# Attention with a gated feed-forward on one core: the projection weights' powers of two applied at the PSUM eviction instead of in the exponential

## The chip, the cores and the metric

The kernel runs on 1 core of one Trainium2 chip. The metric is device time in microseconds (us) from the start to the end of one execution; the number quoted for a kernel is the median of its runs. Besides the runs that are only timed there is one profiled execution, from which every row and trace answer comes.

## The reference

`x` is 2048 x 512, there are 32 heads of 128, with 2048 cached keys and values each, and a feed-forward layer of width 1792. All inputs are bf16.

```python
xn = layernorm(x)                                    # eps 1e-5, no weights
q = (xn @ wq) split into 32 heads of 128
scores = q @ k_cache^T * 128 ** -0.5                 # per head, 2048 x 2048
o = softmax(scores) @ v_cache
s = (heads of o side by side) @ wo                   # 2048 x 4096 @ 4096 x 512
h = relu(xn @ w1 + b1) ** 2
g = silu(h @ w2 + b2)
out = x + s * g
```

## The kernel before

**Tiling.** The 2048 queries are cut into four query blocks of 512 (`j` = 0 to 3). A block passes through all 32 heads, so there are 128 units, numbered `g` = 32 j + head; the text calls such a unit a head. A head has eight steps, numbered `pi` = 8 g + k from 0 to 1023, and a step covers 256 keys:

- two score matmuls of 128 x 512 on TensorE (PE) write keys by queries into half of the PSUM tile `psA`, which has two such halves (`gen_scores`);
- one exponential of 128 x 1024 on ScalarE (ACT) reads that half and writes bf16 into one of eight slots of `pT`. No maximum is subtracted. The score matmuls two steps later need the half that it frees;
- two steps later the value matmuls read the slot (`gen_pv`).

**Two forms of the value product.** In most heads V is the stationary operand and the 512 columns of `pT` move (`gen_pv_b`, 16 matmuls of 512 columns for a head). The sum of the exponentials, which the softmax divides by, is then made beside PE: for a step either VectorE (DVE) reduces the `pT` slot (`den_part`), or GpSimd (POOL) first adds its two halves into `h_sum` (`part_add`) and DVE reduces that (`part_half`). Then come a sum, a small transpose, two trips through device memory and a reciprocal, ACT's copy of the result from PSUM (`o_col`) and a POOL multiplication into `oT`. In the other heads V moves and `pT` is stationary (`gen_pv`, 64 matmuls of 129 columns for a head, the 129th being ones, which gives the sum directly); DVE copies the result (`o_un`), POOL scales it and a DMA transposes it into `oT`. A head of this kind spares DVE and POOL the reductions. Its V is loaded in pieces of 128 elements rather than 512.

**Projection.** In block 0 each head's queries come from four matmuls of 128 x 512 and one DVE copy into `qt_sb`. From block 1 on (g >= 32) two heads are projected together by `job_pair`, with seven block products instead of eight, in Strassen's manner: sums and differences of weight blocks in fp16, which POOL prepares once during blocks 0 and 1 (`wp_sums`), times sums and differences of the activations. So that the fp16 sums keep their precision, each head's weights are first multiplied by a power of two taken from their largest magnitude (`chunk_scale`, `wp_mul`), and this factor has to be undone later. `sc_q[:, head, 1]` holds the factor, and `sc_q[:, head, 0]` its inverse times 128 ** -0.5. In the kernel before, the exponentials of blocks 1 to 3 take `sc_q[:, head, 0]` as their scale, a per-partition operand (a pointer); those of block 0 have the constant 128 ** -0.5.

The products of `job_pair` land in the two banks of `psF`, in steps `n` = 0 to 6. Steps 0, 2 and 4 are copied from PSUM into `u_t` (`keep`), steps 1, 4 and 6 are added to such a copy into `qt_sb` (`add`), step 5 is copied straight into `qt_sb`. Each of these seven evacuations frees a bank for a later step.

**Order.** A Python scheduler writes out each engine's instruction order before the launch. It keeps a planned clock per engine, `_cost` giving each instruction a planned duration. `PE` runs the steps with other jobs between (projections, feed-forward, output projection), at most two or three matmul groups a step (`fill_one`), and a pair's step starts only if its bank is planned to be free (`soon`). DVE's and POOL's other work is put where the planned clocks leave room (`fill_dve`, `fill_pool`). `at_a(g)` decides whether V moves in head g: always in the first two and the last three heads, otherwise where DVE's planned debt (`owed`) passes `A_OWED` and none of the three heads before has V moving. So a change of `_cost` moves instructions on all engines. `copy_off` picks ACT for a copy if ACT's planned clock is within `ACT_ROOM` (500 ns) of PE's, otherwise DVE; in the kernel before all 192 of its copies go to DVE.

Of the kernel before, what the change touches and what calls it, by code (L numbers as in the profile page):

```python
# [5 lines left out]
ACT = mybir.ActivationFunctionType  # L6
ALU = mybir.AluOpType
# [54 lines left out]
def _cost(name, fn):  # L62
    f, k = fn.func, fn.keywords
    n = _elements(k["out"])
    if name == "PE":
        return n / 2.4 + 2.5, n / 2.4 + 166
    if name == "ACT":
        return n * 0.83 + 70, n * 0.83 + 172
    if name == "POOL":
        if f in (_tt, _stt) and n > 1:  # L70
            c = n * 2.3 + 55 if k["out"].tensor.name in ("oT", "out_t") or (
                k["out"].dtype == F16) else n * 2.05 + 60
            return c, c + 50
        return (500, 560) if f is _tt else (n + 100, n + 150)
    if f in (_reduce_t, _abs_max):
        n = _elements(k["in_"])
    elif f is _reduce:
        n = _elements(k["in_"]) * 1.3 + 35
    elif f is _recip:
        n = n * 3.1  # L80
    elif f in (_bn_stats,):
        n = _elements(k["in_"])
    elif f is _ts and _in_sbuf(k["in0"]):
        n = n / 2
    elif f is _tt and k["out"].dtype == F16:
        n = n / 2
    return n / 0.96 + 70, n / 0.96 + 150


# [224 lines left out]
def bass_recurrent_scan__mha_block_cached__dense_activation_squared_relu__prompt_kernel(  # L314
# [14 lines left out]
    _, H, Sk, Dh = A_k_cache.shape  # L329
# [10 lines left out]
    SM_SCALE = float(Dh) ** -0.5  # L340
# [3 lines left out]
    HC = 8  # L344
# [12 lines left out]
    LATE_U = 700  # L357
# [14 lines left out]
    AC = S.eng("ACT")  # L372
    DV = S.eng("DVE")
# [4 lines left out]
    def E(eng, fn, deps=(), inc=True, late=LATE):  # L378
        if eng is DV and backfill[0] is not None:
            backfill[0](S.ready(deps) + late)  # L380
        return S.emit(eng, fn, deps=deps, inc=inc)

    sb = nc.alloc_sbuf_tensor
    NSL, NSW, NQS, NPT, NOT, NOC, NHS = 3, 4, 5, 8, 21, 5, 3
# [19 lines left out]
    u_t = sb("u_t", [P, 3, HB], F32)  # L404
# [5 lines left out]
    sc_q = sb("sc_q", [P, H, 2], F32)  # L410
# [95 lines left out]
    def choose(g, stationary_v):  # L506
# [3 lines left out]
        else:  # L510
# [7 lines left out]
                            op0=ALU.is_equal), deps=[t_idf])  # L518
# [240 lines left out]
    t_cs = {}  # L759
# [38 lines left out]
    def chunk_scale(q):  # L798
        def small(o, i, s1, s2, op0, op1, deps, cast=False):
            out, in0 = mx_t[0:HC, o:o + 1], mx_t[0:HC, i:i + 1]  # L800
            if cast:
                out, in0 = out.bitcast(I32), in0.bitcast(I32)
            return E(DV, partial(_ts, out=out, in0=in0, scalar1=s1, scalar2=s2, op0=op0, op1=op1),
                     deps=deps)

        t = E(DV, partial(_reduce_max, out=mx_t[0:HC, 0:1], in_=mx_h[0:HC, :]),
              deps=[t_mg[q], t_cs.get(q - 1)])
        t = small(1, 0, 1e-30, 1.6e38, ALU.max, ALU.min, [t])
        t = small(2, 1, 0x7F800000, None, ALU.bitwise_and, ALU.bypass, [t], True)
        t2 = E(DV, partial(_recip, out=mx_t[0:HC, 4:5], in_=mx_t[0:HC, 2:3]),  # L810
               deps=[t, t_cp.get(q - 1)])
        t_cs[q] = small(3, 2, SM_SCALE, None, ALU.mult, ALU.bypass, [t, t2, t_cp.get(q - 1)])

    def scale_put(q):
        t_cp[q] = S.emit_dma(SP, partial(_dma, out=sc_scr[q], in_=mx_t[0:HC, 3:5]), sl_cp,
# [83 lines left out]
    def gen_scores(pi):  # L899
        g, k = divmod(pi, NPR)  # L900
        s2, i = pi % 2, g % NSL
        assert t_kfill[g] is not None and t_evac[g] is not None
        t = None
        if g == 0:
            qt, b = divmod(pi, 2)
            for c in range(NKT // 2):
                t = E(PE, partial(_mm_shared, out=psA[:, s2 * 1024 + c * P:s2 * 1024 + (c + 1) * P],
                                  lhsT=kT[:, 0, (b * NKT // 2 + c) * P:(b * NKT // 2 + c + 1) * P],
                                  rhs=qt_sb[:, 0, qt * P:(qt + 1) * P], start=True, stop=True),
                      deps=[t_k0[b], t_q0[qt], t_exp[pi - 2] if pi >= 2 else t_b1[0]],  # L910
                      inc=(c == NKT // 2 - 1))
        else:
            for n in range(2):
                tt = 2 * k + n
                t = E(PE, partial(_mm, out=psA[:, s2 * 1024 + n * 512:s2 * 1024 + (n + 1) * 512],
                                  lhsT=kT[:, i, :].rearrange("p (k t) -> p t k", t=NKT)[:, tt, :],
                                  rhs=qt_sb[:, g % NQS, :],
                                  start=True, stop=True),
                      deps=[t_exp[pi - 2] if pi >= 2 else None, t_kfill[g], t_evac[g],
                            t_bankF[0] if pi == 0 else None],  # L920
                      inc=(n == 1))
        if k == NPR - 1:
            t_S_last[g] = t
        if pi >= NPT and is_b((pi - NPT) // NPR) and pi - NPT not in t_part:
            x = [x for x in quiet if x[1].func is den_part and x[1].args[0] == pi - NPT][0]
            run_quiet(x)
        cuts = [0, QB, 2 * QB] if pi == NPAIR - 1 else [0, 2 * QB]
        for c0, c1 in zip(cuts, cuts[1:]):
            t_exp[pi] = E(AC, partial(_act, out=pT[:, pi % NPT, c0:c1],
                                      in_=psA[:, s2 * 1024 + c0:s2 * 1024 + c1],  # L930
                                      func=ACT.Exp,
                                      scale=SM_SCALE if g < H else sc_q[:, g % H, 0:1]),
                          deps=[t, t_PV[pi - NPT] if pi >= NPT else None, t_part.get(pi - NPT),
                                None if g < H else t_sq[g % H // HC]])
            t_exp0.setdefault(pi, t_exp[pi])

    t_exp0 = {}
# [420 lines left out]
            return t_evac[g]  # L1358
        return NDC, mm, evac

    def copy_off(out, in_, deps):
        if max(AC.t, S.ready(deps)) <= PE.t + ACT_ROOM:
            return E(AC, partial(_act, out=out, in_=in_, func=ACT.Copy), deps=deps)
        return E(DV, partial(_copy, out=out, in_=in_), deps=deps, late=LATE_U)

    def job_pair(g):
        j, p = g // H, g % H // 2
        js = j % 2 * QB
        w, ws = parts(wq_pair[p % 2])

        def x_of(k, q):
            return lambda c: xnT[:, 2 * k + c, js + q * HB:js + (q + 1) * HB]

        def s_of(i):
            return lambda c: xs_t[:, i, c, :]

        steps = [(0, w[0, 0], x_of(0, 0), True), (1, w[0, 1], x_of(1, 0), True),
                 (0, ws[1], s_of(1), False), (1, ws[0], s_of(0), True),
                 (0, ws[2], s_of(2), False), (0, w[1, 1], s_of(3), False),
                 (1, ws[3], x_of(1, 1), False)]  # L1380

        def q_of(g, q):
            return qt_sb[:, g % NQS, q * HB:(q + 1) * HB]

        def mm(n, bank):
            y, lhs, rhs, start = steps[n]
            b = bank ^ y
            place = bankF(b)[:, 0:HB]
            for c in range(2):
                t = E(PE, partial(_mm_shared, out=place, lhsT=lhs[:, c, :], rhs=rhs(c),  # L1390
                                  start=start and c == 0, stop=c == 1),
                      deps=[t_wqfill[g], t_xs[j], t_bankF[b]] + tok_xT[j], inc=c == 1)

            def keep(i):
                t_us[i] = copy_off(u_t[:, i, :], place, [t, t_us[i]])
                return t_us[i]

            def add(x, q, i):
                t_us[i] = E(DV, partial(_tt, out=q_of(x, q), in0=place2, in1=u_t[:, i, :],
                                        op=ALU.add),  # L1400
                            deps=[t, t_us[i], t_S_last[x - NQS]], late=LATE_U)
                return t_us[i]

            place2 = bankF(bank ^ 1)[:, 0:HB]
            if n in (0, 2, 4):
                t_bankF[b] = keep(n // 2)
            if n == 1:
                t_bankF[b] = add(g, 0, 0)
            if n == 4:
                t_bankF[b ^ 1] = add(g + 1, 1, 2)  # L1410
            if n == 5:
                t_bankF[b] = t_evac[g + 1] = copy_off(q_of(g + 1, 0), place,
                                                      [t, t_S_last[g + 1 - NQS]])
            if n == 6:
                t_bankF[b] = t_evac[g] = add(g, 1, 1)
                t_pdone[g] = t_xuse[j] = t
                n_xuse[j] += 1

        def evac(bank, step):
            bank_no[0] ^= 1  # L1420
            if g % H == H - 2 and j + 1 < NQB:
                x_sums(j + 1)
            return t_bankF[bank]
        return 7, mm, evac
# [494 lines left out]
```

## Time and profile before

| | us |
|---|---|
| median of 3 runs | 1223.91 (1222.3 to 1225.86) |
| the profiled execution, its own time | 1221.36 |
| its span, first to last instruction | 1219.5 |
| PE busy | 1205.0 |
| ACT busy | 1148.5 |
| DVE busy | 1089.2 |
| POOL busy | 1072.4 |
| mean granted TensorE clock | 1.000 |

PE is TensorE's matmuls, PEld its weight loads, which overlap matmuls; DVE is VectorE, ACT ScalarE, POOL GpSimd and SP the queue that issues most DMAs. A group's row has its source line, engine, operation, what it writes and reads (out<-in) with shapes, the count; then busy us and mean ns of one; then the engine's idle us just before such instructions and who ended it. Most matmuls have the line of a helper, L231 or L236, so groups are told apart by tile: `psA` scores, `psO` values, `psF` everything else. A line of the wait view reads: who waited, for whom, us in total, times, longest. A line of the stretches has the window, then busy us (and instructions) of PE, PEld, DVE, ACT and POOL, the granted clock, the DMA engines' share and GB/s.

### The profile page before, as it was taken

To read this page: it belongs to the slowest core of one execution; us is meant where nothing else is said; L and a number is where in the kernel's file an instruction comes from. 1 tells how busy PE (TensorE), PEld (TensorE's weight loads), DVE (VectorE), ACT (ScalarE), POOL (GpSimd) and SP (SyncE) were. 2 spreads that over 40 slices of the span, in tenths; PEclk is the share of its full clock that TensorE was granted. 3 is DMA by queue.
4 is the path that set the end of the run, shared out by engine and by line. 5 is a ranking of instruction groups with operands and counts; after the bars stand their busy time and mean duration, and the time that the engine had idled before them with its cause. 6 is when DMAs were issued, how large, how long until landed. Compare 5 with 4: busy or idle time off the path is not lost.

```text
span 1219.5 us, 20766 instructions
## 1 busy us (share of the span) xinstructions
PE 1205.0 (99%) x6716; PEld 699.6 (57%) x6845; DVE 1089.2 (89%) x2064; ACT 1148.5 (94%) x1188; POOL 1072.4 (88%) x1027
## 2 busy tenths in 40 slices
PE   9999999999999999999999999999999999999999
PEld 7555555555665555566566565655555565555566
DVE  5999899998989999977988999798999999989973
ACT  7999999999999999999999999999999999999995
POOL 2999899999879899978977979799999989999973
PEclk9999999999999999999999999999999999999999
DMA  9799999899889799897987879787797887878871
GB/s 218 170 210 213 222 216 208 204 203 225 217 203 240 190 224 208 199 214 170 208 175 177 205 184 210 165 203 181 168 209 179 196 194 166 205 174 188 189 174 42
DMA packets 501023, 236.27 MB, mean 194 GB/s; under 512 B 387985, under 2 KB 477329, under 8 KB 500913
## 3 DMA queue, kind: packets, MB, share of 16 engines
q1 hardware_dynamic: 498816, 230.85, 84.5%
q0 software_dynamic: 1424, 3.81, 1.0%
q8 instruction: 54, 0.88, 0.3%
q14 instruction: 57, 0.46, 0.1%
q10 hardware_dynamic: 672, 0.26, 0.1%
HBM read 152.87 MB, written 11.55 MB: 135 GB/s over the span
## 4 chain that ended last, share of the span: by engine, by line
PE 89%; DVE 3%; ACT 3%; POOL 2%; issue 1%; DMA 0%; SPq 0%; POOLq 0%; ACTq 0%
PE psA L231 33%; PE psO L231 28%; PE psF L231 17%; PE psF L236 6%; PE psO L236 5%; ACT pT L240 2%; DVE d_part L299 2%; POOL h_sum L244 1%; ACT o_col L240 0%; DMA kT<-in_A_k_cache_dram 0%; DVE h2T L254 0%; DVE r_t L250 0%; PE psA L236 0%; POOL wq_sb L244 0%; POOL oT L244 0%
## 5 line engine op out<-in xcount | busy, mean ns | idle before, releaser
L240 ACT ACTIVATE pT<-psA,sc_q 128x1024 bf16<-128x1024 f32 (+1 forms) x769 | 823.5, 1119 | 30.5 <-PE psA L231 25.0
L244 POOL TENSOR_TENSOR h_sum<-pT 128x512 f32<-128x512 bf16 x660 | 748.1, 1160 | 66.4 <-ACT pT L240 45.6
L231 PE MATMUL psA<-qt_sb,kT 128*128 128x512 bf16 x1966 | 593.6, 381 | 5.5 <-ACT pT L240 1.5
L231 PE MATMUL psO<-pT,v_sb 128*128 128x512 bf16 x1737 | 519.8, 379 | 2.2
L299 DVE TRANSPOSE_TENSOR_REDUCE d_part<-h_sum 128x16 f32<-128x512 f32 x660 | 438.5, 681 | 21.5 <-POOL h_sum L244 21.2
L231 PEld LDWEIGHTS psA<-qt_sb,kT 128*128 128x128 bf16 x2032 | 278.1, 145 | 181.3 <-ACT pT L240 37.5
L299 DVE TRANSPOSE_TENSOR_REDUCE d_part<-pT 128x32 f32<-128x1024 bf16 x228 | 275.3, 1213 | 4.9 <-ACT pT L240 4.1
L240 ACT ACTIVATE pT<-psA 128x1024 bf16<-128x1024 f32 x256 | 257.7, 1026 | 22.1 <-PE psA L231 14.5
L231 PEld LDWEIGHTS psO<-pT,v_sb 128*128 128x128 bf16 x1776 | 173.7, 98 | 161.6 <-issue 0.3
L231 PE MATMUL psF<-wo_all,oT 128*128 128x512 bf16 x466 | 155.4, 379 | 0.7
L244 POOL TENSOR_TENSOR oT<-o_col,r_all 128x512 bf16<-128x512 f32 x111 | 142.1, 1281 | 12.4 <-DMA r_all<-r_scr 12.3
L236 PEld LDWEIGHTS psO<-v_sb,pT 128*128 128x128 bf16 x1088 | 72.4, 98 | 23.7 <-issue 0.4
L236 PE MATMUL psO<-v_sb,pT 128*128 128x129 bf16 x1088 | 83.6, 220 | 0.1
L231 PE MATMUL psF<-w_sb,h2T 128*128 128x512 bf16 x220 | 73.9, 379 | 0.2
L231 PE MATMUL psF<-xnT,w_sb 128*128 128x512 bf16 x220 | 73.4, 379 | 0.1
L231 PEld LDWEIGHTS psF<-wo_all,oT 128*128 128x128 bf16 x480 | 46.9, 98 | 40.0
L236 PE MATMUL psF<-xs_t,wq_sb 128*128 128x256 f16 x384 | 68.0, 273 | 0.3
L240 ACT ACTIVATE o_col<-psO 128x512 f32<-128x512 f32 x111 | 66.0, 594 | 0.0
L258 DVE COPY u_t<-psF 128x256 f32<-128x256 f32 x144 | 57.4, 399 | 8.0 <-PE psF L236 7.5
L244 DVE TENSOR_TENSOR qt_sb<-psF,u_t 128x256 bf16<-128x256 f32 x144 | 57.2, 398 | 6.1 <-PE psF L236 5.1
L236 PE MATMUL psF<-xnT,wq_sb 128*128 128x256 bf16 x288 | 53.9, 273 | 0.8 <-DVE h2T L254 0.4
L236 PEld LDWEIGHTS psF<-xs_t,wq_sb 128*128 128x128 f16 (+1 forms) x384 | 35.8, 98 | 29.7 <-DVE u_t L258 2.6
(86 smaller groups left out, 760.8 us busy)
## 6 DMA issues: line engine op xcount, KB each, us to landing
v_sb<-in_A_v_cache_dram SPq DMA_DIRECT2D x508, 128.0 KB, 3.1
r_all<-r_scr SPq DMA_DIRECT2D x111, 256.0 KB, 4.0
wq_sb<-wq_scr SPq DMA_DIRECT2D x48, 448.0 KB, 4.7
wo_all<-in_A_wo_dram SPq DMA_DIRECT2D x64, 256.0 KB, 3.6
wq_scr<-wq_sb SPq DMA_DIRECT2D x16, 448.0 KB, 3.8
wq_sb<-in_A_wq_dram SPq DMA_DIRECT2D x16, 256.0 KB, 4.1
kT<-in_A_k_cache_dram SPq DMA_TRANSPOSE x254, 4.0
wq_sb<-in_A_wq_dram SPq DMA_DIRECT2D x31, 128.0 KB, 3.7
```

The lines of the kernel that those rows point to most:

```text
L231: return e.matmul(out, lhsT, rhs, start=start, stop=stop)
L236: return e.matmul(out, lhsT, rhs, start=start, stop=stop, skip_group_check=True)
L240: return e.activation(out, in_, func, bias=bias, scale=scale)
L244: return e.tensor_tensor(out, in0, in1, op)
L258: return e.tensor_copy(out, in_)
L299: return e.tensor_reduce(out, in_, axis=AX.X, op=ALU.add, apply_transpose=True)
```

## The change

The inverse power of two is taken out of the exponential and applied where the block products leave PSUM. `sc_q[:, head, 0]` becomes the plain inverse; all exponentials have the constant scale. The 144 copies into `u_t` and the 48 into `qt_sb` become multiplications by `sc_q[:, head, 0]` (`scaled`; still all on DVE), and the 144 additions become one multiply-and-add each (`_stt`). These instructions now wait for the load of `sc_q`, the exponentials no longer. `_cost` learns that a pointer operand takes longer, 93 ns more on ACT and 58 elements (60 ns) more on DVE, so the plan is drawn anew: by the built order V moves in 22 heads instead of 17 (before: 0, 1, 12, 28, 32, 37, 42, 55, 59, 64, 69, 74, 81, 103, 125 to 127; after: 0, 1, 8, 28, 32, 36, 40, 45, 52, 56, 62, 66, 74, 80, 84, 88, 98, 103, 110, 125 to 127).

```diff
@@ _cost
+    ap = any(not isinstance(k.get(x, 0.0), (int, float, type(None)))
+             for x in ("scale", "scalar", "scalar1"))
     if name == "ACT":
-        return n * 0.83 + 70, n * 0.83 + 172
+        c = n * 0.83 + (163 if ap else 70)
+        return c, c + 102
...
+    n += 58 if ap else 0
     return n / 0.96 + 70, n / 0.96 + 150
@@ chunk_scale
-        t_cs[q] = small(3, 2, SM_SCALE, None, ALU.mult, ALU.bypass, [t, t2, t_cp.get(q - 1)])
+        t_cs[q] = small(3, 2, 1.0, None, ALU.mult, ALU.bypass, [t, t2, t_cp.get(q - 1)])
@@ gen_scores
-                                      scale=SM_SCALE if g < H else sc_q[:, g % H, 0:1]),
-                          deps=[t, t_PV[pi - NPT] if pi >= NPT else None, t_part.get(pi - NPT),
-                                None if g < H else t_sq[g % H // HC]])
+                                      scale=SM_SCALE),
+                          deps=[t, t_PV[pi - NPT] if pi >= NPT else None, t_part.get(pi - NPT)])
@@ job_pair
-    def copy_off(out, in_, deps):
+    def scaled(out, in_, scale, deps):
         if max(AC.t, S.ready(deps)) <= PE.t + ACT_ROOM:
-            return E(AC, partial(_act, out=out, in_=in_, func=ACT.Copy), deps=deps)
-        return E(DV, partial(_copy, out=out, in_=in_), deps=deps, late=LATE_U)
+            return E(AC, partial(_act, out=out, in_=in_, func=ACT.Copy, scale=scale), deps=deps)
+        return E(DV, partial(_ts, out=out, in0=in_, scalar1=scale, scalar2=None, op0=ALU.mult),
+                 deps=deps, late=LATE_U)
...
-            def keep(i):
-                t_us[i] = copy_off(u_t[:, i, :], place, [t, t_us[i]])
+            def back(x):
+                return sc_q[:, x % H, 0:1]
+
+            def keep(i, x):
+                t_us[i] = scaled(u_t[:, i, :], place, back(x), [t, t_us[i], t_sq[g % H // HC]])
...
-                t_us[i] = E(DV, partial(_tt, out=q_of(x, q), in0=place2, in1=u_t[:, i, :],
-                                        op=ALU.add),
-                            deps=[t, t_us[i], t_S_last[x - NQS]], late=LATE_U)
+                t_us[i] = E(DV, partial(_stt, out=q_of(x, q), in0=place2, scalar=back(x),
+                                        in1=u_t[:, i, :], op0=ALU.mult, op1=ALU.add),
+                            deps=[t, t_us[i], t_S_last[x - NQS], t_sq[g % H // HC]], late=LATE_U)
```

The calls follow: `keep(n // 2, g + n // 4)`, and `scaled(q_of(g + 1, 0), place, back(g + 1), ...)` in step 5.

More of the change, by code (lines that the diff above doesn't have):

```diff
@@ L1405, in mm @@
             if n in (0, 2, 4):
-                t_bankF[b] = keep(n // 2)
+                t_bankF[b] = keep(n // 2, g + n // 4)
             if n == 1:
@@ L1411, in mm @@
             if n == 5:
-                t_bankF[b] = t_evac[g + 1] = copy_off(q_of(g + 1, 0), place,
-                                                      [t, t_S_last[g + 1 - NQS]])
+                t_bankF[b] = t_evac[g + 1] = scaled(
+                    q_of(g + 1, 0), place, back(g + 1),
+                    [t, t_S_last[g + 1 - NQS], t_sq[g % H // HC]])
             if n == 6:
```

## The prediction

> **What bounds the kernel now.** I read four views of the profile, in this order. First the busy time per engine, then the stretches.
>
> ```profile
> PE 1205.0 (99%) x6716; PEld 699.6 (57%) x6845; DVE 1089.2 (89%) x2064; ACT 1148.5 (94%) x1188; POOL 1072.4 (88%) x1027
> ```
>
> ```profile
> 50.00:300.00 250.00, 248.66 (x1233) 136.12 (x1256) 235.80 (x432) 233.40 (x258) 238.91 (x234) 1.00 0.96 210
> 300.00:400.00 100.00, 99.16 (x580) 58.41 (x589) 91.47 (x175) 96.69 (x101) 84.64 (x87) 1.00 0.95 218
> 400.00:500.00 100.00, 97.83 (x520) 55.25 (x530) 93.73 (x178) 97.41 (x104) 92.57 (x93) 1.00 0.92 211
> 600.00:900.00 300.00, 297.63 (x1646) 174.38 (x1678) 271.67 (x523) 289.28 (x291) 267.37 (x246) 1.00 0.81 187
> 900.00:1200.00 300.00, 297.56 (x1599) 171.78 (x1629) 270.76 (x518) 288.73 (x293) 276.28 (x250) 1.00 0.79 181
> ```
>
> The columns are busy us of PE, PEld, DVE, ACT, POOL, then clock, DMA share and GB/s. PE has nearly no idle time and the granted clock is 1.00 everywhere. The page draws a 512-column matmul 379 ns long, though in the trace's start times unhindered matmuls follow each other every 215.83 ns (512 columns), 109.16 (256), 56.66 (129) and 55.8 (128). So a busy PE hides short waits, and I add up slots instead. Before, there are 4872 matmuls of 512, 688 of 256, 1088 of 129 and 197 narrow ones: 1051.5 + 75.1 + 61.6 + 11.0 = 1199.2 us. The first matmul starts at 1.0 and 2.8 us follow the last one's slot. The span is 1219.5, so 16.5 us are waits of PE. By start times 3.7 of them lie in the first 50 us, 0.7 in the rest of query block 0 (to 307 us), and 6.2, 2.5 and 3.3 in blocks 1, 2, 3 (to 609, 906 and the end). Those 12.0 us of blocks 1 to 3 are all that this change can remove. Who causes them? The waits, asked for each block (total us, times, longest):
>
> ```profile
> PEld psA L231 <- ACT pT L240: 3.3, 11, 0.5
> ...
> PEld psA L231 <- ACT pT L240: 17.2, 55, 0.7
> ...
> PEld psA L231 <- ACT pT L240: 7.6, 33, 0.6
> ...
> PEld psA L231 <- ACT pT L240: 9.4, 38, 0.6
> ```
>
> These are blocks 0 (from 50 us), 1, 2 and 3. The score matmuls' weight loads wait for ACT's exponential to free the psA buffer, much more often from block 1 on. (A weight load runs ahead of its matmul, so its wait is longer than PE's loss.) Why from block 1?
>
> ```profile
> L240 ACT ACTIVATE pT<-psA,sc_q 128x1024 bf16<-128x1024 f32 x767 | 822.4, 1121 | 30.5 <-PE psA L231 25.0 <-PE psO L231 0.5 <-POOL h_sum L244 0.4
> L240 ACT ACTIVATE pT<-psA 128x1024 bf16<-128x1024 f32 x256 | 257.7, 1026 | 22.1 <-PE psA L231 14.5 <-PE psA L236 1.7
> L240 ACT ACTIVATE wq_sb<-wq_sb,sc_q 128x512 bf16<-128x512 bf16 x32 | 23.3, 729 | 0.1
> L240 ACT ACTIVATE th_t<-z_t 128x512 f32<-128x512 f32 x16 | 10.2, 638 | 0.0
> L258 DVE COPY u_t<-psF 128x256 f32<-128x256 f32 x144 | 57.4, 399 | 8.0 <-PE psF L236 7.5
> L244 DVE TENSOR_TENSOR qt_sb<-psF,u_t 128x256 bf16<-128x256 f32 x144 | 57.2, 398 | 6.1 <-PE psF L236 5.1
> L258 DVE CAST qt_sb<-psF 128x512 bf16<-128x512 f32 x30 | 20.1, 669 | 5.4 <-PE psF L231 3.5 <-PE psA L231 1.6
> L250 DVE TENSOR_SCALAR r_t<-psF,b1f 128x512 bf16<-128x512 f32 x56 | 40.2, 718 | 6.0 <-PE psF L231 5.6
> L254 DVE SCALAR_TENSOR_TENSOR h2T<-psF,b1f,r_t 128x512 bf16<-128x512 f32 x56 | 41.9, 748 | 1.7
> L244 DVE TENSOR_TENSOR acc<-psF,acc 128x512 f32<-128x512 f32 x28 | 18.7, 667 | 4.8 <-PE psF L231 4.7
> ```
>
> The exponential with a per-partition scale takes 1121 ns, with a constant 1026: 95 ns more. The 512-wide pair (729 with sc_q, 638 without) says 91. Back to back, exponentials start 996 ns apart with the scale and 903 without (10th percentiles). A step of the loop, two score and two value matmuls plus its share of the rest, has 1153 ns of PE slots on average in block 1 (the built order's matmuls times the slots above) and 862 where it has no other work. An extra ACT instruction, 478 ns from start to start for o_col every eighth step and 613 for the wq_sb scalings that last until 504 us, takes 478 / (1153 - 996) = 3 steps or more to catch up; with 903 it takes two.
>
> **Part by part.** *The exponential* loses its pointer in 769 instructions: 767 x 95 ns = 73 us of ACT. ACT lies beside PE, so this is worth only PE's waits. I take them down to block 0's, where the constant form already runs: 0.7 us a block, 2.1 for three. To that I add 1.0, the positive waits of psF projections in blocks 1 to 3 today, which ACT does not cause. So 12.0 becomes 3.1 before the new costs: -8.9. Bounds: -12.0 (no wait left) and 0 (all filled by something else).
>
> *The evacuations.* 192 copies from psF (144 u_t, 48 qt_sb) become a multiply by a pointer, and 144 adds become multiply-and-add. No row has these at 256 columns. The nearest rows are at 512: r_t over the cast, 718 - 669 = 49 ns, and h2T over acc, 748 - 667 = 81. DVE gets 192 x 49 + 144 x 81 = 21 us more. They hold a psF bank that the pair's next matmuls need; ahead of them stand S and PV matmuls. The wait view names u_t or qt_sb as PE's releaser at L236 19 times, 4.7 us. At 81 ns longer each that is 1.5 us at most and nothing at least, if the matmuls placed ahead absorb it; I take 0.8, the middle. Behind these instructions DVE holds the denominators' reductions, for which POOL and the pT slots wait; they are 8 slots deep, and ACT waited 0.4 us for d_part in all. Below nothing is possible only if DVE is otherwise relieved, which is the next part.
>
> The Trainium skill, "VectorE: DVE Perf Modes", in its table of errata-adjusted cycles, prices a PSUM source at 120 cycles plus the elements with no term for a pointer scalar: 392 ns at 256 columns (an estimate from that page), near the 399 row, and the multiply would then be free. The two 512-wide rows speak against that; with the page's price the 0.8 would be 0.
>
> *The new wait.* The evacuations now wait for sc_q, as the exponentials did. Its last load is issued at 325.7 us and lands 4.2 us later; the heads of that last chunk are projected some 170 steps into block 1, about 510 us. Nothing queues for it: 0.
>
> *Five more heads with V moving* (17 to 22; by the built order they are 0, 2, 1 and 2 more in blocks 0 to 3). PE: 320 matmuls of 129 come, 320 x 56.66 = 18.1 us; 80 of 512 go, 80 x 215.83 = 17.3. That is +0.9 us on the path (unrounded). DVE loses 24 x 0.681 + 16 x 1.213 of reductions and 5 x 1.05 of sum, turn, total and reciprocal, 41 us, and gains 10 x 0.421 + 5 x 0.178, 5 us. So DVE as a whole falls by 15 us, the pointers included. POOL loses 24 x 1.160 + 5 x 1.281 and gains 5 x 1.042: -29 us. SP loses 20 small DMAs and gains 5 transposes; as many V loads are issued, in shorter pieces, and they land in 6.1 us at worst while issued two heads (19 us) ahead. No wait of PE in the trace names them: 0. Three heads without V moving lie between each pair of chosen ones as before, and heads after a moving one show no more PE waits than others (0.67 us at head 43, but 0.84 at 39).
>
> *The small rest* (a factor 1.0 in place of 1/sqrt(128) in four 8-element instructions) is 0.
>
> Sum: -8.9 + 0.8 + 0.9 = -7.2 us. The profiled execution of 1221.4 us (span 1219.5 and 1.9 around it) would be 1214.2, its span 1212.3; it stood 2.5 us under the median of 1223.9, which becomes 1216.7.
>
> **Rivals.** *The waits change hands.* From head 8 on every engine's order is planned anew, and PE's single waits are accidents of an order (0.5 us for a psF bank at 413 us). If they come back behind DVE or POOL, 5 to 12 of the 12 us remain with the 0.9: 1218 to 1225, no change at the middle. Against it: DVE and POOL both get lighter. *Slower: the bank.* In each of 48 pairs seven evacuations hold a psF bank while the pair's next step needs it; 336 in all. If PE pays the whole 81 ns, that is 27 us. For slower by 0.3% (3.7 us) it must eat the gain of 8.0 too: 11.7 us or 144 of the 336; at 200 of them 16 us, so 1223.9 - 8.0 + 16 = 1232. For it: DVE is busy 89% and serves in order. Against it: PE waits there 19 times now. *It isn't the pointer.* If the 95 ns came from block 1's company in PSUM, nothing is gained: 1223.9 + 0.9 + 0.8 = 1225.6. The 729 against 638 ns, SBUF to SBUF, speaks against it.
>
> **The numbers.** My forecast 0.74, waits that change hands 0.13, the bank 0.11, not the pointer 0.02. A measurement of this kernel tells about 0.3% (3.7 us) from no change. Faster is my case: 0.74; the same are the second and the last: 0.15; slower 0.11. The low end has no wait left: 1223.9 - 12.0 + 0.9 = 1212.8, less 1.8 for the spread of three runs (1222.3 to 1225.9). The high end reaches into waits that change hands, 1222; beyond lie the rest of that case and the bank, under 0.2.
>
> **What would show it.** Right: all 1023 exponentials of 1024 columns at about 1026 ns; ACT near 1075 us busy; PE's waits on ACT at psA under 12 us in place of 37.5; u_t multiplies near 450 ns and the multiply-adds near 480; 1408 matmuls of 129. Wrong: waits at psF L236 for DVE above 10 us (the bank), or PE's waits in block 1 still near 6 us under another releaser, or exponentials still at 1121.

## The result and the profile after

The changed kernel takes 1216.8 us (median, 1215.9 to 1217.9), the kernel before 1223.7: a ratio of 0.9943, 95% interval 0.9925 to 0.996. Beside other kernels it later gave 1216.2 and 0.9942 (0.993 to 0.9954). The prediction said 1216.7. The experiments below show that the cause it named is right, and that the number came out as close as it did because errors of several terms cancelled.

Busy time, then the stretches, of the changed kernel (columns as before: busy us of PE, PEld, DVE, ACT, POOL):

```profile
PE 1201.2 (99%) x6952; PEld 711.7 (59%) x7085; DVE 1074.1 (88%) x2019; ACT 1095.4 (90%) x1183; POOL 1044.5 (86%) x1008
```

```profile
50.00:300.00 250.00, 247.01 (x1224) 135.03 (x1248) 237.26 (x430) 231.22 (x256) 234.87 (x229) 1.00 0.94 207
300.00:400.00 100.00, 98.88 (x629) 60.82 (x639) 89.98 (x176) 92.41 (x102) 88.12 (x92) 1.00 0.97 225
400.00:500.00 100.00, 99.41 (x537) 57.84 (x547) 92.72 (x174) 94.01 (x106) 90.99 (x92) 1.00 0.90 212
...
600.00:900.00 300.00, 297.90 (x1704) 177.59 (x1737) 268.96 (x511) 272.53 (x291) 259.00 (x241) 1.00 0.84 187
900.00:1200.00 300.00, 297.97 (x1717) 177.50 (x1750) 263.43 (x498) 271.41 (x291) 260.61 (x238) 1.00 0.79 180
```

ACT is busy 53 us less, DVE 15 and POOL 28, all beside a PE that is full either way. (Both traces lack some matmul records, 6716 of 6845 before and 6952 of 7085 here, counted against the weight loads, so the busy times of PE are a little low; the changed kernel's second trace has all 7085 and 1208.0 us.) PE gains most where it lost most: 97.83 of the 100 us from 400 on became 99.41. But from 50 to 300 us, where the kernel's instructions hardly differ, it went from 248.66 down to 247.01.

The weight loads' waits on ACT, for blocks 0 (from 50 us), 1, 2 and 3:

```profile
PEld psA L235 <- ACT pT L244: 5.9, 14, 1.3
...
PEld psA L235 <- ACT pT L244: 4.0, 14, 0.4
...
PEld psA L235 <- ACT pT L244: 1.9, 8, 0.4
...
PEld psA L235 <- ACT pT L244: 3.5, 13, 0.5
```

Blocks 1 to 3 fall from 34.2 us to 9.4; block 0 rises from 3.3 to 5.9. The groups that were in question:

```profile
L244 ACT ACTIVATE pT<-psA 128x1024 bf16<-128x1024 f32 x1023 | 1028.5, 1026 | 99.4 <-PE psA L235 69.4 <-POOL h_sum L248 1.6 <-PE psA L240 1.6
...
L253 DVE TENSOR_SCALAR u_t<-psF,sc_q 128x256 f32<-128x256 f32 x144 | 65.8, 457 | 5.8 <-PE psF L240 4.6
L258 DVE SCALAR_TENSOR_TENSOR qt_sb<-psF,sc_q,u_t 128x256 bf16<-128x256 f32 x144 | 65.2, 453 | 4.8 <-PE psF L240 3.6
```

The exponentials of 1024 columns now all take 1026 ns, and ACT mostly waits for PE (69.4 us before them, 39.5 before the change). On DVE the multiply with a pointer takes 58 ns more than the copy (457 - 399) and the multiply-add 55 ns more than the addition (453 - 398). At 512 columns most of such a step is the pointer: in this trace a multiply-add by a constant (`z_t`) takes 678 ns, one by a pointer (`h2T`) 746, a plain addition (`acc`) 675. For the multiply no row has a constant beside it.

Single executions of one kernel differ by 2 to 5 us, in two of the experiments by 6.6 and 7.4: the profiled one of before lies 2.4 us under its later median of 26 runs (1223.8), that of the changed kernel 1.1 us over its own. So kernels are compared by medians, and the profile says where waits lie. Below, PE's waits are counted as in the prediction, by start times less slots; the experiments of the last rows, too, are told in the next section.

| us of PE's waits | first 50 us | block 0 | 1 | 2 | 3 | matmul slots | median |
|---|---|---|---|---|---|---|---|
| before | 3.7 | 0.7 | 6.2 | 2.5 | 3.3 | 1199.3 | 1223.8 |
| changed | 4.2 | 2.8 | 2.1 | 1.6 | 1.4 | 1200.1 | 1216.8 |
| changed, again | 3.8 | 2.2 | 2.0 | 1.4 | 1.6 | 1200.1 | 1216.2 |
| e1 | 3.9 | 2.0 | 2.9 | 1.3 | 2.0 | 1199.3 | 1217.0 |
| e2 | 3.7 | 1.8 | 6.8 | 4.1 | 5.1 | 1199.3 | 1227.1 |
| e3 | 4.2 | 3.0 | 4.4 | 3.3 | 4.3 | 1199.3 | 1224.0 |
| e4 | 4.1 | 2.4 | 5.9 | 2.6 | 3.6 | 1200.1 | 1223.0 |
| f1 | 3.6 | 0.7 | 2.5 | 1.3 | 2.6 | 1199.3 | 1215.8 |
| f2 | 3.9 | 1.2 | 5.6 | 4.4 | 4.5 | 1200.1 | 1226.4 |
| g1 | 4.0 | 2.9 | 2.8 | 1.1 | 1.4 | 1200.1 | 1217.0 |
| h3 | 3.7 | 3.0 | 3.7 | 1.7 | 2.0 | 1199.6 | 1218.8 |
| h2 | 3.9 | 4.3 | 3.6 | 1.4 | 5.2 | 1199.3 | 1230.5 |
| t4 | 4.1 | 5.0 | 4.3 | 1.9 | 1.5 | 1200.0 | 1217.6 |
| r1 | 3.7 | 1.6 | 6.5 | 3.0 | 2.8 | 1198.9 | 1221.9 |

### The profile page after: what moved, and what is told of

Its sections match the earlier page's. It is cut to its first block, busy times and chain, and to the rows that moved or that the text cites. A ratio compares the mean times of both kernels' runs of the same rounds, so it can differ in the third digit from the quotient of the medians.

```text
span 1216.0 us, 21110 instructions
## 1 busy us (share of the span) xinstructions
PE 1201.2 (99%) x6952; PEld 711.7 (59%) x7085; DVE 1074.1 (88%) x2019; ACT 1095.4 (90%) x1183; POOL 1044.5 (86%) x1008
## 4 chain that ended last, share of the span: by engine, by line
PE 94%; DVE 2%; DMA 2%; issue 1%; POOL 1%; SPq 0%; ACT 0%; ACTq 0%; DVEq 0%; POOLq 0%
PE psA L235 35%; PE psO L235 29%; PE psF L235 18%; PE psO L240 6%; PE psF L240 6%; DVE d_part L303 1%; DMA wq_sb<-in_A_wq_dram 1%; POOL h_sum L248 1%; DMA kT<-in_A_k_cache_dram 0%; SPq L311 0%; DMA wq_sb<-wq_scr 0%; PE psA L240 0%; ACT pT L244 0%; DVE qt_sb L258 0%; POOL acc L248 0%
## 5 line engine op out<-in xcount | busy, mean ns | idle before, releaser
L244 ACT ACTIVATE pT<-psA 128x1024 bf16<-128x1024 f32 x1025 | 1029.5, 1025 | 99.4 <-PE psA L235 69.4
L248 POOL TENSOR_TENSOR h_sum<-pT 128x512 f32<-128x512 bf16 x636 | 720.5, 1158 | 75.9 <-ACT pT L244 53.4
L235 PE MATMUL psO<-pT,v_sb 128*128 128x512 bf16 x1659 | 496.4, 379 | 2.6 <-DVE o_un L262 0.3
L303 DVE TRANSPOSE_TENSOR_REDUCE d_part<-h_sum 128x16 f32<-128x512 f32 x636 | 423.0, 682 | 12.8 <-POOL h_sum L248 12.3
L235 PEld LDWEIGHTS psA<-qt_sb,kT 128*128 128x128 bf16 x2032 | 277.2, 145 | 167.1 <-ACT pT L244 15.3
L303 DVE TRANSPOSE_TENSOR_REDUCE d_part<-pT 128x32 f32<-128x1024 bf16 x212 | 256.1, 1212 | 3.8 <-ACT pT L244 3.1
L240 PEld LDWEIGHTS psO<-v_sb,pT 128*128 128x128 bf16 x1408 | 93.9, 98 | 34.9 <-issue 0.4
L240 PE MATMUL psO<-v_sb,pT 128*128 128x129 bf16 x1408 | 108.2, 220 | 0.1
L253 DVE TENSOR_SCALAR u_t<-psF,sc_q 128x256 f32<-128x256 f32 x144 | 65.8, 457 | 5.8 <-PE psF L240 4.6
L240 PE MATMUL psF<-xs_t,wq_sb 128*128 128x256 f16 x384 | 69.7, 273 | 0.1
L258 DVE SCALAR_TENSOR_TENSOR qt_sb<-psF,sc_q,u_t 128x256 bf16<-128x256 f32 x144 | 65.2, 453 | 4.8 <-PE psF L240 3.6
L262 DVE COPY o_un<-psO 128x258 f32<-128x258 f32 x44 | 16.7, 420 | 50.1 <-PE psO L240 50.1
L240 PEld LDWEIGHTS psF<-xs_t,wq_sb 128*128 128x128 f16 (+1 forms) x384 | 36.8, 98 | 30.2 <-DVE u_t L253 3.6
L240 PE MATMUL psF<-xnT,wq_sb 128*128 128x256 bf16 x288 | 53.8, 273 | 0.4 <-DMA wq_sb<-wq_scr 0.4
```

The costliest lines, as they stand in the source:

```text
L235: return e.matmul(out, lhsT, rhs, start=start, stop=stop)
L240: return e.matmul(out, lhsT, rhs, start=start, stop=stop, skip_group_check=True)
L244: return e.activation(out, in_, func, bias=bias, scale=scale)
L248: return e.tensor_tensor(out, in0, in1, op)
L253: return e.tensor_scalar(out, in0, scalar1=scalar1, scalar2=None, op0=op0)
L258: return e.scalar_tensor_tensor(out=out, in0=in0, scalar=scalar, in1=in1, op0=op0, op1=op1)
```

## The experiments

**First set: the two edits apart, in the old plan and in the new.** e1 is the kernel before with one edit:

```diff
-                                      scale=SM_SCALE if g < H else sc_q[:, g % H, 0:1]),
+                                      scale=SM_SCALE),
```

> The kernel before, in its own order on every engine, with the constant scale in all exponentials and no power of two undone at the eviction: the scores of blocks 1 to 3 keep the heads' factors, which leaves out that part of the computation. Main theory: the pointer in the exponential is the whole cause, so PE's waits in blocks 1 to 3 fall from 12.0 us to about 3 with no new cost on DVE and PE's slots unchanged: 8.9 us faster than before, about 1214.8. Waits change hands: the order of before keeps its accidents, 5 to 12 of the 12 us stay, 1217 to 1224. Not the pointer: exponentials still near 1121 ns in blocks 1 to 3 and no change, 1223.7.

Measured: 1217.0 us, ratio 0.9947 (0.9935 to 0.9959). The pointer in the exponential alone was worth 6.8 us, of 8.9 forecast. The wait view of e1:

```profile
PEld psA L231 <- ACT pT L240: 13.4, 39, 1.2
PEld psF L236 <- DVE h2T L254: 2.9, 6, 1.2
PEld psF L236 <- DVE u_t L258: 2.6, 11, 0.3
PEld psF L236 <- DVE qt_sb L244: 2.2, 9, 0.5
```

The first line was 37.5 us in 137 waits; the others are what they were in the kernel before:

```profile
PEld psF L236 <- DVE h2T L254: 2.7, 6, 0.8
PEld psF L236 <- DVE u_t L258: 2.6, 11, 0.3
PEld psF L236 <- DVE qt_sb L244: 2.1, 8, 0.5
```

So the waits did not change hands. By their tiles in the two traces, PE, DVE, ACT and POOL execute the same instructions in the same order as before, so the length of the exponential is what differs.

e3 is the changed kernel with the old `_cost`, hence the old plan (in the traces of both, these four engines have the order of before); e2 is e3 with the pointer scale put back into the exponential:

```diff
@@ e3, e2: _cost as before
-    n += 58 if ap else 0
...
@@ e2 also
-                                      scale=SM_SCALE),
+                                      scale=SM_SCALE if g < H else sc_q[:, g % H, 0:1]),
...
```

> The kernel before, in its own order on every engine, with the evictions of the block products multiplying by the pointer, while the exponentials keep the pointer scale too: both apply the inverse power of two and the 128 ** -0.5, so the scores of blocks 1 to 3 are scaled twice. Main theory: only DVE's 336 evictions are longer, by 49 to 81 ns, and PE pays 0 to 1.5 us, 0.8 by the sum: 1224.5. The bank rival: 16 us or more, 1240. If DVE's extra 21 us (and nothing taken off it here, as no head is changed) also delays the reductions that free pT, PE's waits on ACT at psA grow by some us: 1226 to 1229.

> The changed kernel with the cost function of before, so the order of every engine and the 17 heads with V moving are those of before: constant scale in the exponentials, pointer multiplies on DVE, the reference's output. Main theory, adding up: -8.9 + 0.8 and no 0.9 for the heads, so 8.1 us faster than before, 1215.6, about 1 us faster than the changed kernel. If the plan matters (it does not know of DVE's 21 us more), DVE falls behind and the kernel stands 2 to 5 us slower than the changed one, 1219 to 1222.

Measured: e2 1227.1 us, ratio 1.003 (1.0019 to 1.004); e3 1224.0, ratio 1.000 (0.9991 to 1.001). In the old plan DVE's pointers cost 3.3 us with the slow exponential and 7.0 with the fast one (e3 against e1): the whole gain is given back. The wait view of e3:

```profile
PEld psA L231 <- ACT pT L240: 13.1, 34, 1.8
PEld psF L236 <- DVE u_t L249: 9.6, 39, 0.6
PEld psF L236 <- DVE qt_sb L254: 8.5, 31, 0.8
PEld psF L231 <- DVE qt_sb L249: 4.0, 15, 0.5
PEld psF L236 <- DVE h2T L254: 2.1, 6, 0.5
```

ACT is waited for no more than in e1 (13.1 against 13.4 us), but the psF banks are: 25.8 us in 96 waits, all lines for DVE together, against 9.0 in 31 in e1. In e2, too, it is these waits that grow (24.4 us against 9.7 before), while those on ACT at psA do not (34.8 against 37.5); its time lies in the range of the third theory, but not by that theory's cause. This is the bank rival at a quarter of its full price: 7.0 us is 21 ns for each of the 336 evacuations, which are 55 to 58 ns longer.

e4 is the changed kernel in its own order with the pointer back in the exponential; `_cost` leaves `Exp` out, so that the plan stays:

```diff
-        c = n * 0.83 + (163 if ap else 70)
+        c = n * 0.83 + (163 if ap and k["func"] is not ACT.Exp else 70)
@@ gen_scores: scale and deps as before the change
```

> The changed kernel in its own order on every engine, 22 heads, with the pointer scale back in the exponentials of blocks 1 to 3 (the inverse power of two is applied again there, and the 128 ** -0.5 is left out, so those scores are scaled differently). Main theory: the 8.9 us come back, as PE waits for ACT in blocks 1 to 3 again: 1225.6, and the block 1 waits of PE by start times are near 6 us. Waits change hands: the new order has less of them whatever the exponential takes, as DVE and POOL are lighter: 1219 to 1222. In block 0, which this edit does not touch, ACT stood twice for 1.1 us before a weight scaling whose load had not landed; the two waits come again if they belong to this order, and not if they were chance in that execution.

Measured: 1223.0 us, ratio 0.9997 (0.9986 to 1.0007), against 1216.2 to 1216.8 without the pointer: 6.2 to 6.8 us, as in e1, and 8.9 were forecast. Its waits on ACT at psA were 15.3 us in 49 in the changed kernel, whose order these four engines have:

```profile
PEld psA L235 <- ACT pT L244: 43.0, 149, 1.6
```

The exponential's share is the same in both plans; the new plan alone, with the slow exponential, brings 4.1 us against e2 and nothing that can be told apart against the kernel before.

**Second set: what in the new plan is worth 7.2 us (e3 to the changed kernel)?** It knows of the pointers' time, and it has five heads more with V moving. f1 and f2 take these apart with a fixed list of heads in `at_a`:

```diff
@@ f1: the new _cost, the 17 heads of before; f2: the old _cost, the 22 heads of after
-            a_set[g] = g < FIRST_B or g >= NG - 3 or (...)
+            a_set[g] = g in [0, 1, 12, 28, ...]
```

> The changed kernel with its new cost function, but V moving in the 17 heads of before, by a fixed list. The runs so far: exponential alone 1217.0, the changed kernel in the old plan 1224.0, in its own plan 1216.8. So the new plan is worth 7.2 us, where the prediction had it cost 0.9. Theory A, the bank's due time: what helps is that the planner knows an evacuation to be 60 ns longer and puts the pair's next matmuls later; then this one stands near 1217, with the waits of psF's weight loads on DVE under 9 us. Theory B, the load on DVE: what helps are the five heads more that take 36 us off DVE; then this one stands near 1223, with waits of psF on DVE near 20 us.

> The changed kernel with the cost function of before, but V moving in the 22 heads of the changed kernel, by a fixed list. Theory A (due time): near 1224, the 22 heads alone do not help, the waits of psF on DVE stay near 20 us, and the heads cost 0.9 by slots. Theory B (load on DVE): near 1217 to 1218.

Measured: f1 1215.8 us, ratio 0.9939 (0.9927 to 0.9951); f2 1226.4, ratio 1.0022 (1.0013 to 1.0031). The whole gain goes with the planned time, and the heads bring nothing: f2 is even 2.4 us slower than e3. The wait views, f1 and then f2, each beside 3.6 and 1.0 us for the same two tiles in the changed kernel:

```profile
PEld psF L240 <- DVE u_t L253: 3.6, 19, 0.3
...
PEld psF L240 <- DVE qt_sb L258: 1.5, 6, 0.6
```

```profile
PEld psF L236 <- DVE qt_sb L254: 11.7, 43, 0.8
PEld psF L236 <- DVE u_t L249: 11.3, 46, 0.6
```

How the plan may do it can be counted in the built orders. For the 240 evacuations whose bank the same pair needs again, there lie between the matmuls that fill the bank and the next ones that need it emptied, by slots, 1618 ns of other PE work on average in the old plan (median 1727) and 1551 in f2, the slowest; but 1708 in f1, 1726 in h3 below and 1735 in the changed kernel (median 1945 in these three): a planned 60 ns seems to tip `soon`, so that another piece of work goes first. Where DVE puts the evacuation among its reductions changes too; the two were not told apart.

g1 is the changed kernel's own order with the plain copies and adds (`_cost` adds the 58 elements to them, so the plan stays):

```diff
-        return E(DV, partial(_ts, out=out, in0=in_, scalar1=scale, scalar2=None, op0=ALU.mult),
-                 deps=deps, late=LATE_U)
+        return E(DV, partial(_copy, out=out, in_=in_), deps=deps, late=LATE_U)
...
-                t_us[i] = E(DV, partial(_stt, ...
+                t_us[i] = E(DV, partial(_tt, out=q_of(x, q), in0=place2, in1=u_t[:, i, :],
+                                        op=ALU.add),
```

> The changed kernel in its own order on every engine (22 heads, the evacuations planned 60 ns longer), but the evacuations are the plain copies and adds of before: no power of two is undone anywhere, so the scores of blocks 1 to 3 keep the heads' factors. Against the changed kernel it shows what the pointers on DVE cost where the plan knows of them. Theory A: the plan covers them, 0 to 1 us, so 1216 to 1217. Theory B (what counts is DVE's total): 21 us of DVE less, and 1 to 3 us faster, 1214 to 1216.

Measured: 1217.0 us, ratio 0.994 (0.9927 to 0.9952). In a plan that allows for them, the pointers on DVE cost nothing that can be measured. And g1 takes what e1 takes, 1217.0: without the pointers the two orders, heads included, are equally good. So the 7.2 us are no gain of the new order as such; they are what the pointers on DVE cost where the plan does not know of them.

**Third set: how much must the plan know, and can it be better?** h3 has the old `_cost` and 60 ns for the 336 evacuations alone, which gives 19 heads with V moving:

```diff
+    sc = k.get("scalar", k.get("scalar1"))
+    n += 58 if hasattr(sc, "tensor") and sc.tensor.name == "sc_q" else 0
```

> The changed kernel with the cost function of before and one thing added: 60 ns for the 336 evacuations that multiply by sc_q, and nothing for any other instruction with a pointer (r_t, h2T, xn_t, the weight scalings). The planner then chooses 19 heads with V moving. If the banks' due times of the pair job are what the new plan is worth, it stands as the changed kernel does, 1216 to 1218, and the waits of psF's weight loads on u_t and qt_sb stay under 8 us. If half of it came from knowing r_t, h2T and the rest, it stands between, 1219 to 1221.

Measured: 1218.8 us (1217.9 to 1220.2), ratio 0.9962 (0.9949 to 0.9975): 5.2 of the 7.2 us, between the two forecasts. The rest may be r_t and h2T, whose pointers it does not plan, or chance of the order: PE's waits are over the changed kernel's mainly in block 1 (3.7 against 2.1 us), where its weight loads wait 6.9 us on ACT at psA (4.0 in the changed kernel) and 1.2 on u_t and qt_sb.

h2 is f1 with twice the time planned:

```diff
-    n += 58 if ap else 0
+    n += 116 if ap else 0
```

> The changed kernel with V moving in the 17 heads of before and with 121 ns instead of 60 planned for a DVE instruction's pointer (measured: 55 to 58 more than the plain copy or add). No time on any engine changes but by the order. If a plan needs only to be no shorter than what happens, it is the same as with 60, 1215.8 within 1 us. If margin pays (the remaining waits of psF on DVE, 6 us in the weight-load view, go), 1 to 2 us faster. If a plan that is too long costs, PE's jobs bunch up later and it is 1 to 4 us slower.

Measured: 1230.5 us (1223.7 to 1231.1), ratio 1.0044 (1.0029 to 1.006): 14.7 us slower than f1 with the same instructions in another order, far over the 1 to 4 us forecast for a plan that is too long. Its bank waits are few, with 1820 ns of other PE work on average by the count above, but ACT is waited for longer, at psA:

```profile
PEld psA L235 <- ACT pT L244: 26.8, 72, 2.2
PEld psO L235 <- issue: 3.1, 5, 1.4
PEld psF L240 <- DVE u_t L253: 3.1, 17, 0.6
```

The profiled execution is the shortest of its seven, 6.8 us under the median. Of the 8.0 us by which it exceeds f1's profiled one, 3.6 are waits of PE in block 0, 1.1 in block 1 and 2.6 in block 3. Where the longer ones lose the rest is open: the mean granted clock was 0.997 to 0.999 in five of the six, but 1.000 in the sixth (1230.9 us), and 0.1 to 0.3% of 1224 us would be 1.2 to 3.7 us, an estimate. Every plan here is a single order, so a part of such differences can be chance of the order.

Two attempts at a better version. t4 holds the weight scalings back until 1 us after their load's planned landing (21 heads with V moving); r1 lets ACT take more of the copies (99 of the 192, 15 heads). Both orders are planned anew:

```diff
@@ t4
-    WQ_PACE = 22
+    WQ_PACE = 21
...
-            HALF_SLACK if fn.func is part_half else 0)
+            HALF_SLACK if fn.func is part_half else 1000 if fn.func is wp_mul else 0)
@@ r1
-    ACT_ROOM = 500
+    ACT_ROOM = 1000
```

> The changed kernel, with the weight scalings that ACT does in blocks 0 and 1 put 1 us later after their load's planned landing (and the pairs' preparation started every 21 instead of 22 steps, so that the last one is still in time); the plan is drawn anew, with 21 heads. In the changed kernel's profile ACT stood twice for 1.1 us before such a scaling, and PE lost 2.0 us of block 0 behind it; in three other kernels with this preparation 2 or 3 such waits of 1.1 to 2.4 us showed. If the load's landing is the cause, no such wait of ACT is left, block 0's waits of PE fall from 2.8 to about 1 us, and it stands 1 to 2 us under the changed kernel, 1215. If they only move to another head, no gain, 1216 to 1218.

> The changed kernel with ACT_ROOM at 1000 instead of 500 ns: 99 of the 192 evacuations that are copies go to ACT, which the change has relieved by 53 us (1148.5 to 1095.4 busy), and the planner chooses 15 heads with V moving. By slots PE's matmuls are 1.2 us shorter (7 heads x 0.17). If ACT's room is real, 0.5 to 2 us faster than the changed kernel, 1215 to 1216. If ACT's in-order work delays exponentials again, PE's waits on ACT at psA grow and it is 1 to 5 us slower.

Measured: t4 1217.6 us (1215.7 to 1222.3), ratio 0.9948 (0.9934 to 0.9962), not told apart from the changed kernel; two waits of ACT on a weight load remain, 1.3 us together, and its profiled execution, the longest of its six, has one wait of 4.0 us in block 0 on DVE's `acc`. r1 1221.9, ratio 0.9988 (0.998 to 0.9997): 5 to 6 us slower than the changed kernel. ACT is busy 1119.1 us there, and PE's waits on it double:

```profile
PEld psA L235 <- ACT pT L244: 31.8, 89, 0.8
```

So ACT's 10% of idle time was no room for these copies. That a copy between two exponentials delays the second, as a longer exponential does, fits the doubled waits, but r1's plan and heads differ as well, and this was not taken apart.

> The changed kernel once more, beside the others on one chip: 1216.8 within 1 us. Its second profile tells whether the two waits of ACT on a weight load in block 0 (2.2 us, PE lost 2.0) belong to the order: then they come at the same heads, 11 and 22; or to chance: then elsewhere or not at all.

Measured: 1216.2 us. ACT waited once for a weight load, 1.7 us at head 11; head 22's wait did not come again. No version is faster than the changed kernel beyond the spread of the runs: f1, at 1215.8, is within it.

## Why the prediction was right, and where not

- **The bound and its cause: right.** PE's slots and its waits on ACT at psA set the time, and the pointer made them (e1, e4). **The size was too large:** -8.9 in the sum, -6.2 to -6.8 measured. The term that was mis-sized is what stays in blocks 1 to 3: 2.1 us, by block 0's 0.7 a block, plus 1.0 for psF, 3.1 in all; in e1 6.2 us stayed (2.9, 1.3, 2.0). The step that failed is taking block 0's wait for the floor of the others: f1, whose block 0 has 0.7 again, keeps 6.4 in blocks 1 to 3, and the changed kernel 5.0 to 5.1. The 0.7 was no firm number either: in e1 to e3, whose block 0 is the same, it was 1.8 to 3.0, with weight loads that landed late (last section). What the 5 to 6 us consist of was not taken apart. (The 862 ns of a step without other work are 863 by the prediction's own slots; nothing rests on it.)
- **The evacuations, +0.8: the value held, the reason did not.** The pointers' time was right (49 to 81 ns forecast, 55 and 58 measured), and with the new plan they cost nothing (g1). But the step took them as if the order stood still, with 19 waits that grow, 1.5 us at most; with the order standing still they cost 3.3 to 7.0 us (e2, e3), and the 19 waits at L236 became 65 and 70. What was a just sufficient distance became a wait, which the bound left out. The bank rival was a real mechanism, at 21 ns an evacuation and not 81. It did not decide because the change also tells the planner.
- **The new plan, taken as 0 besides the heads: this step failed.** Its order is worth 7.2 us against the same change in the old one, all of it the price of the pointers that it hides (e1 and g1 are equal). The prediction named `_cost` but valued it only by the heads it moves.
- **The heads, +0.9: agrees in sign, not shown in size.** 17 heads in the new plan are 0.3 to 0.9 us faster than 22, which is within the spread, and in the old plan 22 cost 2.4 us more than 17. The 0.9 itself is a count of slots.
- **The sum: met partly by luck.** Step by step the runs give -6.8 for the exponential (before to e1), +7.0 for the pointers in the old order (e1 to e3) and -7.2 for the new order with its heads (e3 to the changed kernel): -7.0, with -6.9 to -7.7 measured directly. The forecast had -8.9, +0.8 and +0.9. So its gain was 2.1 too large, its cost of the pointers 6.2 too small, and its part for the new order 8.1 off on the other side, and these cancel. By the other way round, from e1 to g1 (0.0) and on to the changed kernel (-0.2 to -0.8), a gain that was 2 us too large met two costs, of 0.8 and 0.9, that do not show in the times.
- **What would show it:** of the marks set, the exponentials at 1026 ns and the 1408 matmuls of 129 came, and none of the signs of being wrong: the waits at psF L240 for DVE stayed under 10 us, and block 1 has 2.1 us of waits. The multiplies took 457 and the multiply-adds 453 ns, against 450 and 480. The psA waits came to 15.3 us, not under 12, and ACT was busy 1095 us, not 1075, since the busy time counts overlapping instructions once: before, the 767 exponentials of 1121 ns, 859.8 us, made 822.4 us of busy time, and now the 1023 of 1026 ns, 1049.6 us, make 1028.5.

The Trainium skill's page "VectorE: DVE Perf Modes" has no pointer term in its table of errata-adjusted cycles. For the plain form that table gives 392 ns at 256 columns, an estimate, near the 398 to 399 measured. The forms with a pointer took 55 to 58 ns more, and in the old order PE paid 3.3 to 7.0 us for them (e2, e3), where the page's price would make it nothing: here the measurement decides.

## What to carry to other kernels

Where a planner writes out the schedule, change its durations together with the instruction. Here the same 336 longer instructions, each in front of a PSUM bank that PE needs again, cost 7.0 us in the order planned without their extra time and nothing measurable in the order planned with it. Test the new instruction in the old order too, since that shows what is at stake. A longer planned time is not a safer one: twice the extra time gave an order 14.7 us slower.

Idle time of an engine does not say that its instructions are free. ACT was 94% busy, and PE waits for it at the two halves of `psA`; 95 ns less on each of 767 exponentials, 73 us of ACT, brought 6 to 7 us.

Before using a residual wait as a floor, read it from more than one execution, and from a stretch that does the same work.

## What the runs showed of the hardware that was not expected

A weight scaling whose load had not landed held up ACT, and the exponential that stands behind it in ACT's order started only after it: in the changed kernel's trace ACT stood 1.07 us from 112.3 us on, and PE then 0.80:

```profile
113.36 0.72 ACT L244 ACTIVATE wq_sb<-wq_sb,sc_q 128x512 bf16<-128x512 bf16 x1 [1.07 <-DMA wq_sb<-in_A_wq_dram]
...
113.99 1.00 ACT L244 ACTIVATE pT<-psA 128x1024 bf16<-128x1024 f32 x1
...
115.05 0.66 PE L235 MATMUL psA<-qt_sb,kT 128*128 128x512 bf16 x2 [0.80 <-ACT pT L244]
```

Such waits came to 0.5 to 2.4 us in the profiles of the other kernels and to 0.13 in that of before. They belong partly to the order and partly to the execution: in the four profiles with the changed kernel's order (its own two, e4 and g1) one at head 11 always came, of 0.4 to 1.7 us, and a second of 1.1 to 1.4 at head 22 once, at head 27 twice and once not at all. Holding the scalings back did not clearly remove them.
